# The last expert rows: gated activations as the stationary operand, in two column groups

## The chip, the cores and the metric

The kernel runs on one core of a Trainium2 chip. The metric is the device time of one execution in microseconds. Times inside an execution come from one profiled execution of the kernel before, counted from the start of its span.

## The reference

The reference is one attention block with 16 query heads on one shared key and value head, followed by a block that sends only the 8 best of 2048 rows through a gated expert and adds the result to those rows.

```python
S, D, F, C = 2048, 448, 1792, 8
h = x + softmax(q k^T / sqrt(28)) v @ wo          # on layernorm(x), 16 heads of 28
x2 = layernorm(h)
r = x2 @ w_r
idx = argsort(-r)[:8]
g = silu(x2[idx] @ w_gate)                        # 8 x 1792
u = x2[idx] @ w_up
y = (g * u) @ w_down                              # 8 x 448
out = h + x2
out[idx] += y * sigmoid(r[idx])
```

The change is in the last lines: the product with `w_down`, the sum with the eight residual rows, and the write of the eight sums over their rows of the output.

## The kernel before

The 2048 rows lie as 16 tiles of 128 rows in SBUF. The attention's scores are made in pairs of matmuls into two PSUM banks, and their exponentials are taken by ScalarE (L1012) and in part by VectorE with integer operations (L1024, L1031). The products with the values (`P,Vs` and `Y,Vs` in the trace) go in fours to four column groups of TensorE: each writes 32 partitions of PSUM, beginning at 0, 32, 64 and 96. All TensorE matmuls carry the line of the helper `mm`, L436, so the tiles tell them apart.

The program is written as a graph of operations with durations, priorities, and the keys that they read and write. A planner orders each engine's operations by priority and readiness, and turns the dependences into waits on semaphores. Of an operation's waits, the one that the planner expects last is held by the operation's own first instruction, and the others stand ahead of it as instructions of their own (L289).

The tail begins when the last attention block is done. The last four row tiles are normalised (L964 for the expert's input `xn`, L971 for the output rows `x_sb`). The scores of all rows are compared, and `oh5` holds one-hot columns: for each of the last four tiles, 128 x 8 with a one where a row of the tile is the j-th chosen, and a fifth one for the rows that were gathered from earlier tiles (`extc`, which lies in `xnT`). A product with `oh5` therefore picks the chosen rows. The picked inputs go through `wg_sb` and `wu_sb` in 14 blocks of 128 hidden units; the result, gated and weighted with the sigmoid, is `guT`: 128 hidden units x 8 rows for each of 14 blocks, made in two halves (L1218).

Then the part that is changed. `psy` is a set of four banks, one for each quarter of 112 output columns, and holds the sum transposed: output columns on partitions, the 8 rows as columns. `row_mm` (L1181) makes the chosen residual rows, five matmuls a quarter, with 128 columns of the rows as the stationary operand and 8 one-hot columns moving. The down projection (L1222) adds 56 matmuls, 14 a quarter, with 128 columns of `w_down` stationary and 8 columns of `guT` moving. VectorE copies the quarters in two halves to `yT` (L1230), TensorE transposes them back by matmuls with an identity, and ScalarE (L1236) and VectorE (L1238) copy 224 columns each to `fin`, which lies in the tile `wq_sb`. GpSimd scatters the 8 rows of `fin` to the output with an indirect DMA (L1239).

Of the kernel before, what the change touches and what calls it, by code (L numbers as in the profile page):

```python
# [6 lines left out]
ACT = mybir.ActivationFunctionType  # L7
# [3 lines left out]
BF16 = mybir.dt.bfloat16  # L11
# [6 lines left out]
PE, AC, DV, PO, SP = "pe", "act", "dve", "pool", "sp"  # L18
# [282 lines left out]
def _main(nc, G, sb, ps, psb, flag, scr, xs, ptab, A_x, A_wq, A_wk, A_wv, A_wo, B_w_r, B_w_gate, B_w_up, B_w_down, out,  # L301
          exact=False):
    S, D, H, C = A_x.shape[1], A_x.shape[2], 16, 8
    DH = D // H
    FF = B_w_gate.shape[1]
    NT, NQB, CK, NB = S // 128, S // 512, 112, 16
    NCH, NFC = D // CK, FF // 128
    XW = D + 4
# [13 lines left out]
    ident = sb("ident", [128, 128], BF16)  # L322
    idi = sb("idi", [128, 128], I32)
    x_raw = sb("x_sb", [128, NT * XW + 16], BF16)
    x_sb = x_raw[:, 0:NT * XW].rearrange("p (t d) -> p t d", d=XW)
# [44 lines left out]
    outf = x_sb[:, :, 0:D]  # L370
# [6 lines left out]
    wd_raw = sb("wd_sb", [128, NFC * D + 16], BF16)  # L377
    wd_sb = wd_raw[:, 0:NFC * D].rearrange("p (k n) -> p k n", n=D)
    fin = wq_sb[0:8, 0, :]
# [10 lines left out]
    extc = xnF[:, 3072:3072 + XW + 16]  # L390
# [15 lines left out]
    oh5 = sb("oh5", [128, 5, 8], BF16)  # L406
# [8 lines left out]
    onesh = sb("onesh", [128, 128], F16)  # L415
    pz = sb("pz", [128, 8], F16)
    wlo = sb("wlo", [1, 8], F32)
    yT = sb("yT", [128, NCH, 8], BF16)
    xselT = sb("xselT", [128, NCH, 8], BF16)
    eg = sb("eg", [128, NFC, 8], F32)  # L420
    sg = sb("sg", [128, NFC, 8], F32)
    guT = sb("guT", [128, NFC, 8], BF16)
# [3 lines left out]
    def acc_bank(b):  # L426
        return 6 + b % 2
# [4 lines left out]
    def pk(b):  # L432
        return ("ps", b)

    def mm(o, l, r, start, stop):
        return lambda e: e.matmul(o, lhsT=l, rhs=r, start=start, stop=stop)  # L436
# [25 lines left out]
    for i in range(4, NT, 4):  # L462
        dma(x_sb[:, i:i + 4, 0:D], x_v[:, i:i + 4, :], [("x", t) for t in range(i, i + 4)], lat=3500.0 + 400 * i,
            reads=[("x", 3)])
    G.op(PO, lambda e: e.iota(idi[:, :], [[1, 128]], base=0, channel_multiplier=-1), 250, writes=["idi"])
    G.op(PO, lambda e: e.tensor_single_scalar(ident[:, :], idi[:, :], 0, ALU.is_equal), 560,
         reads=["idi"], writes=["ident"])
    G.op(PO, lambda e: e.memset(nhalf[:, :], -0.5), 100, writes=["nhalf"])
    for _ in range(44):
# [3 lines left out]
         writes=["pid2"])  # L473
    G.op(DV, lambda e: e.tensor_single_scalar(pidx[:, :], pidx[:, :], 31, ALU.bitwise_and), 70, reads=["pidx"],
         writes=["pidx"])
    for p in range(2):
        G.op(DV, lambda e, p=p: e.tensor_scalar(ksc[:, p:p + 1], pid2[:, :], 32, KSCALE,
                                                ALU.is_ge if p else ALU.is_lt, ALU.mult), 70, reads=["pid2"],
             writes=[("ksc", p)])
# [3 lines left out]
         writes=["qone"])  # L483
# [3 lines left out]
    def pad_wq(g, after=()):  # L487
# [5 lines left out]
        else:  # L493
# [4 lines left out]
         reads=["wk_sb", "wk_rep"], writes=["wk_rep"])  # L498
    G.op(PO, lambda e: e.tensor_copy(wv_pad[0:CK, :, 1:1 + DH], wv_sb[0:CK, :, :]), 250,
         reads=["wv_sb", "wv_pad"], writes=["wv_pad"])  # L500
# [7 lines left out]
    def kk(j, p):  # L508
        return ("K0", min(j, 2), p) if j < 4 else ("K", j // 4, p)
# [474 lines left out]
    left = [p for p in first if p not in [q[0:2] for q in EARLY]]  # L984
# [96 lines left out]
    if exact:  # L1081
# [4 lines left out]
        for b in range(NB):  # L1086
            if b >= 2:
                q_project(b, misc_bank(b))
            for i in range(4):
                rows = slice(32 * i, 32 * i + 32)  # L1090
                for k in range(4):
# [4 lines left out]
                         reads=[("Q", b % 4), ("Qh", b % 4)] + [kk(j, i % 2) for j in (0, 2, 4, 8, 12)], writes=[pk(c) for c in range(4)])  # L1096
                    G.op(DV, lambda e, r2=r2: e.tensor_reduce(nmax[:, r2:r2 + 1], ps[:, 0:4, :], AX.XY, ALU.max,
                                                              negate=True), 2200,
                         reads=[pk(c) for c in range(4)], writes=[("nmax", r2)])
                    G.op(DV, lambda e, r2=r2: e.tensor_scalar(nmax[:, r2:r2 + 1], nmax[:, r2:r2 + 1], OCT, None,  # L1100
                                                              ALU.mult), 90,
                         reads=[("nmax", r2)], writes=[("nmax", r2)])
                    G.op(AC, lambda e, r2=r2: e.activation(Pq[:, r2, :], ps[:, 0:4, :].rearrange("p a b -> p (a b)"),
                                                           ACT.Exp, bias=nmax[:, r2:r2 + 1], scale=OCT), 1800,
                         reads=[pk(c) for c in range(4)] + [("nmax", r2)], writes=[("Pq", r2)])
                    for hf in range(2):
# [3 lines left out]
                             reads=[("Pq", r2), "ident"], writes=[pk(bank)])  # L1110
                        G.op(DV, lambda e, bank=bank, hf=hf, r2=r2: e.tensor_copy(
                            PT[:, r2, 8 * hf:8 * hf + 8, :].rearrange("p a b -> p (a b)"), psb[:, bank, :]), 1100,
                            reads=[pk(bank)], writes=[("PT", r2, hf)])
                        G.op(PE, [mm(ps[rows, acc_bank(b), k * 128:(k + 1) * 128], Vs[:, 0, j, :], PT[:, r2, j, :],
                                     j == 0, j == NT - 1) for j in range(8 * hf, 8 * hf + 8)], 600,
                             reads=[("PT", r2, hf)] + [("V", c) for c in range(4)] + ["V1"], writes=[pk(acc_bank(b))])
            post_block(b)
    else:
        events.sort(key=lambda t: t[0])
        for t, fn in events:  # L1120
# [7 lines left out]
         writes=["Ls", "bad1"])  # L1128
    G.op(PE, mm(ps[0:1, 2, 32:33], bad1[:, :], ones128[:, :], True, True), 200, reads=["bad1", "ones128"],
         writes=[pk(2)])  # L1130
    G.op(DV, lambda e: e.tensor_copy(flag[:, :], ps[0:1, 2, 32:33]), 120, reads=[pk(2)], writes=["flag"])
    G.op(DV, lambda e: e.engine_nop() if False else e.tensor_copy(bad1[:, :], bad1[:, :]), 70, reads=["bad1", "flag"],
         writes=["bad1"])
# [4 lines left out]
         writes=[pk(0)])  # L1138
    for k in range(4):
        G.op(PE, mm(ps[0:1, 1, k * 128:(k + 1) * 128], x_sb[:, 12 + k, D + 2:D + 3], ident[:, :], True, True), 100,  # L1140
             reads=[("r", 12 + k), "ident"], writes=[pk(1)])
    G.op(DV, lambda e: e.max(top8[:, 1, :], row), 620, reads=[pk(0), pk(1)], writes=[("top8", 1)])
    G.op(DV, lambda e: e.max_index(idx8[:, 1, :], top8[:, 1, :], row), 700, reads=[pk(0), pk(1), ("top8", 1)],
         writes=[("idx8", 1)])
# [5 lines left out]
        writes=["oh5"])  # L1150
    G.prio = 321
    G.op(AC, lambda e: e.activation(wrow[:, :], top8[:, 1, :], ACT.Exp, scale=-1.0), 200, reads=[("top8", 1)],
         writes=["wrow"])
    G.op(DV, lambda e: e.tensor_scalar(wrow[:, :], wrow[:, :], 1.0, None, ALU.add), 70, reads=["wrow"],
         writes=["wrow"], after=[oh_op])
# [3 lines left out]
         writes=["wlo"])  # L1159
    G.op(DV, lambda e: e.tensor_copy(bz[0:1, 1, :], wlo[:, :]), 90, reads=["wlo", "bz"], writes=["bz3"])  # L1160
    G.op(DV, lambda e: e.tensor_tensor(bz[0:1, 2, :], wlo[:, :], bz[0:1, 1, :], ALU.subtract), 90, reads=["wlo", "bz3"],
         writes=["bz4"])
# [1 line left out]
        last_out(k)  # L1164
    G.prio = 312
    psg = ps[:, 7, 0:NCH * 8].rearrange("p (c j) -> p c j", j=8)
    psy = ps[:, 4:8, 0:8]
    fns = []
    for ch in range(NCH):
        for k in range(4):  # L1170
            o = (12 + k) * D + ch * CK
# [6 lines left out]
         reads=["onesb", "bz", "bz2", "bz3", "bz4"], writes=[pk(7)], prio=321.5)  # L1178
    G.op(DV, lambda e: e.tensor_copy(wbc[:, :], ps[:, 7, 64:72]), 70, reads=[pk(7)], writes=["wbc"], prio=324)

    def row_mm(ch, prio):  # L1181
        fns = []
        for k in range(4):
            o = (12 + k) * XW + ch * CK
            fns.append(mm(psy[:, ch, :], x_raw[:, o:o + 128], oh5[:, k, :], k == 0, False))
        fns.append(mm(psy[:, ch, :], extc[:, ch * CK:ch * CK + 128], oh5[:, 4, :], False, False))
        G.op(PE, fns, 140, reads=["oh5", "extc", "extc2", "x_end"] + [("outf", 12 + k) for k in range(4)] +
             [("r", 12 + k) for k in range(4)], writes=[pk(4 + ch)], prio=prio)

    ps3 = ps[0:8, 2, 480:482]  # L1190
    G.op(PE, [mm(ps3, oh5[:, k, :], x_sb[:, 12 + k, D:D + 2], k == 0, False) for k in range(4)] +
# [1 line left out]
         reads=["oh5", "extc2", ("xi", 0), ("xi", 1)], writes=[pk(2)], prio=313)  # L1193
    G.op(DV, lambda e: e.tensor_copy(sel3[:, :], ps3[:, 1:2]), 70, reads=[pk(2)], writes=["sel3"], prio=318)
    G.op(DV, lambda e: e.tensor_tensor(idxc[:, :], ps3[:, 0:1], sel3[:, :], ALU.add), 70,
         reads=[pk(2), "sel3"], writes=["idxc"], prio=318)
    HF = NFC // 2
    pgu = ps[:, 0:4, 0:HF * 8].rearrange("p b (c j) -> p b c j", j=8)
    for h in range(2):
        fcs = range(HF * h, HF * h + HF)  # L1200
        bg, bu = h, 2 + h
        for w_, nm, bk in ((wg_sb, "wg_sb", bg), (wu_sb, "wu_sb", bu)):
            G.op(PE, [mm(pgu[:, bk, fc - HF * h, :], w_[0:CK, ch, fc * 128:(fc + 1) * 128], xselT[0:CK, ch, :], ch == 0,
                         ch == NCH - 1) for fc in fcs for ch in range(NCH)], 780, reads=[nm, "xselT"],
                 writes=[pk(bk)], prio=320 + bk)
        sl = slice(HF * h, HF * h + HF)
        G.op(DV, lambda e, sl=sl, bg=bg: e.tensor_scalar(eg[:, sl, :], pgu[:, bg, :, :], -43.0, None, ALU.max), 130,
             reads=[pk(bg)], writes=[("eg", h)], prio=320)
        for f, sc, bi in ((ACT.Exp, -1.0, 0.0), (ACT.Ln, 1.0, 1.0), (ACT.Exp, -1.0, 0.0)):
            G.op(AC, lambda e, f=f, sc=sc, bi=bi, sl=sl: e.activation(  # L1210
                eg[:, sl, :], eg[:, sl, :], f, bias=bi, scale=sc), 190,
                reads=[("eg", h)], writes=[("eg", h)], prio=325)
        G.op(DV, lambda e, sl=sl, bg=bg: e.tensor_tensor(sg[:, sl, :], pgu[:, bg, :, :], eg[:, sl, :], ALU.mult), 150,
             reads=[pk(bg), ("eg", h)], writes=[("sg", h)], prio=325)
        G.op(DV, lambda e, sl=sl: e.tensor_tensor(sg[:, sl, :], sg[:, sl, :],
                                                  wbc[:, :].unsqueeze(1).broadcast_to([128, HF, 8]), ALU.mult), 150,
             reads=[("sg", h), "wbc"], writes=[("sg", h)], prio=325)
        G.op(DV, lambda e, sl=sl, bu=bu: e.tensor_tensor(guT[:, sl, :], pgu[:, bu, :, :], sg[:, sl, :], ALU.mult), 150,  # L1218
             reads=[pk(bu), ("sg", h)], writes=[("guT", h)], prio=325)
    for ch in range(NCH):  # L1220
        row_mm(ch, 326 + 0.1 * ch)
    for h in range(2):  # L1222
        for c2 in ((0, 1), (2, 3)):
            G.op(PE, [mm(psy[:, ch, :], wd_raw[:, fc * D + ch * CK:fc * D + ch * CK + 128], guT[:, fc, :], False,
                         fc == NFC - 1) for ch in c2 for fc in range(HF * h, HF * h + HF)], 390,
                 reads=[("guT", h), "wd_sb", "wd_end"], writes=[pk(4 + ch) for ch in c2], prio=327 + h)
    G.prio = 330
    for h in range(2):
        c2 = slice(2 * h, 2 * h + 2)
        G.op(DV, lambda e, c2=c2: e.tensor_copy(yT[0:CK, c2, :], psy[0:CK, c2, :]), 100,  # L1230
             reads=[pk(4 + 2 * h), pk(5 + 2 * h)], writes=[("yT", h)])
    for h in range(2):
        G.op(PE, [mm(ps[0:8, h, ch * CK:(ch + 1) * CK], yT[0:CK, ch, :], ident[0:CK, 0:CK], True, True)
                  for ch in (2 * h, 2 * h + 1)], 200, reads=[("yT", h), "ident"], writes=[pk(h)], prio=329.5 if h == 0 else None)
    hd = D // 2
    G.op(AC, lambda e: e.activation(fin[:, 0:hd], ps[0:8, 0, 0:hd], ACT.Identity), 300, reads=[pk(0)],  # L1236
         writes=["fin0"] + wqs)
    G.op(DV, lambda e: e.tensor_copy(fin[:, hd:D], ps[0:8, 1, hd:D]), 300, reads=[pk(1)], writes=["fin1"])  # L1238
    o = G.op(PO, lambda e: e.indirect_dma_start(out[0], bass.IndirectOffsetOnAxis(ap=idxc[:, 0:1], axis=0),  # L1239
                                                fin[:, :], None), 1000, dma=True,  # L1240
             reads=["fin0", "fin1", "idxc"] + [("out", q, k) for q in range(4) for k in (1, 3)],
             writes=[("out", 4)])
# [4 lines left out]
def bass_sequential_preLN__grouped_kv_mqa__moe_arch_mod__prompt_kernel(  # L1247
# [3 lines left out]
    with es:  # L1251
# [13 lines left out]
        for exact in (False, True):  # L1265
            G = _Graph(sems, dsems, graphs[0] if exact else None)
            with contextlib.ExitStack() as mem:
                def sb(name, shape, dt, mem=mem, pre="x_" if exact else ""):
                    return mem.enter_context(nc.sbuf_tensor(pre + name, shape, dt))
                _main(nc, G, sb, ps, psb, flag, scr, xs, ptab, A_x, A_wq, A_wk, A_wv, A_wo, B_w_r, B_w_gate, B_w_up, B_w_down,  # L1270
                      out, exact)
            graphs.append(G)
# [74 lines left out]
```

## Time and profile before

| | |
|---|---|
| median of 3 runs | 388.9 us (388.54 to 389.18) |
| the profiled execution | 387.67 us |
| its span | 385.9 us |
| mean granted TensorE clock | 0.984 |
| busy: PE, DVE, ACT, POOL | 344.0, 338.2, 374.1, 115.0 us |
| instructions | 8129 |

The span runs from the first to the last instruction; the execution's own time is a little longer. Busy times are sums over the span; `PEld` is TensorE's loading of stationary operands, which goes on beside its matmuls. A shape such as `128*8 128x224` names the rows and columns of the stationary operand and then the moving one. In the order of instructions below, a matmul's row shows the tiles read, moving operand first, and the shape of what it writes.

### The profile page before, as it was taken

What the parts mean: (1) busy time and instruction counts of PE and PEld (TensorE: products, weight loads), DVE (VectorE), ACT (ScalarE), POOL (GpSimd) and SP (SyncE); (2) the same over time, 40 slices, a digit from 0 to 9 for tenths busy, and PEclk for the clock granted to TensorE, in tenths of its full rate; (3) what the DMA queues carried; (4) which work ended last, traced back from release to release, by engine and by line L of the source; (5) the groups of instructions that cost most, each with busy time, mean ns of one, the idle gap of its engine ahead of it and who ended that gap; (6) DMA issues with size and microseconds to landing.
All of it is one profiled execution on the core that took longest, in us unless ns stands there. A gap on an engine that the chain in (4) does not pass through costs nothing.

```text
span 385.9 us, 8129 instructions
## 1 busy us (share of the span) xinstructions
PE 344.0 (89%) x3361; PEld 105.6 (27%) x3361; DVE 338.2 (88%) x613; ACT 374.1 (97%) x433; POOL 115.0 (30%) x149
## 2 busy tenths in 40 slices
PE   7799898989988999899998988999898999888945
PEld 7333222222222222222222222222222222222324
DVE  6985888888998999989999989999999998999382
ACT  6999999999999999999999999999999999999992
POOL 7440002544123112404101244402145454431100
PEclk9999999999999999999999999999999999999985
DMA  8696000100000000201001000011001010100011
GB/s 208 163 235 190 2 2 12 49 2 29 2 27 5 4 29 26 77 1 54 2 14 63 7 27 27 28 50 31 26 30 51 3 53 27 52 26 20 14 51 55
DMA packets 18045, 17.12 MB, mean 44 GB/s; under 512 B 6660, under 2 KB 15124, under 8 KB 18004
## 3 DMA queue, kind: packets, MB, share of 16 engines
q1 hardware_dynamic: 17652, 16.32, 14.7%
q8 instruction: 27, 0.44, 0.5%
q10 hardware_dynamic: 288, 0.23, 0.2%
q14 instruction: 14, 0.11, 0.1%
q0 software_dynamic: 64, 0.02, 0.0%
HBM read 11.70 MB, written 4.86 MB: 43 GB/s over the span
## 4 chain that ended last, share of the span: by engine, by line
ACT 92%; PE 3%; DVE 3%; DMA 1%; issue 0%; SPq 0%; POOL 0%; POOLq 0%
ACT P L1012 90%; PE ps L436 3%; DMA wq_sb<-in_A_wq_dram 1%; ACT xn L964 1%; DVE Y L1024 1%; DVE topb L856 0%; DVE bn L934 0%; SPq L449 0%; ACT x_sb L825 0%; DVE Y L1031 0%; ACT xnT L618 0%; POOL out_dram L1239 0%; ACT Rb L741 0%; ACT Rb L739 0%; ACT wq_pad L491 0%
## 5 line engine op out<-in xcount | busy, mean ns | idle before, releaser
L1012 ACT ACTIVATE P<-ps 128x1024 bf16<-128x1024 f32 x388 | 356.3, 1132 | 1.4 <-PE ps L436 1.3
L436 PE MATMUL ps<-Q,K 64*128 64x512 bf16 x1024 | 179.9, 385 | 29.3 <-ACT P L1012 25.0
L1024 DVE TENSOR_SCALAR Y<-ps 128x1024 int16<-128x1024 f32 x124 | 151.2, 1219 | 19.8 <-PE ps L436 19.5
L1031 DVE TENSOR_SCALAR Y<-Y 128x2048 int16<-128x2048 int16 x153 | 100.4, 685 | 0.5
L436 PEld LDWEIGHTS ps<-Q,K 64*128 64x128 bf16 x1024 | 44.7, 93 | 175.4 <-ACT P L1012 152.7
L1031 POOL TENSOR_SCALAR Y<-Y 128x2048 int16<-128x2048 int16 x33 | 62.6, 1898 | 96.4 <-DVE Y L1031 87.6
L436 PE MATMUL ps<-Y,Vs 128*32 128x512 bf16 x992 | 84.9, 383 | 0.0
L436 PE MATMUL ps<-P,Vs 128*32 128x512 bf16 x776 | 76.3, 388 | 0.1
L767 POOL TENSOR_TENSOR On<-Ot,Rb 128x512 bf16<-128x512 f32 x15 | 19.1, 1273 | 45.5 <-DVE Y L1031 30.6
L436 PEld LDWEIGHTS ps<-Y,Vs 128*32 128x32 bf16 x992 | 23.8, 95 | 27.3 <-issue 17.5
L436 PEld LDWEIGHTS ps<-P,Vs 128*32 128x32 bf16 x776 | 19.6, 93 | 42.5 <-issue 41.7
L763 POOL TENSOR_TENSOR Ls<-Ls,Lc 128x16 f32<-128x16 f32 x15 | 4.2, 280 | 68.2 <-DVE Y L1031 60.9
L436 PE MATMUL ps<-xnT,wq_pad 112*128 112x512 bf16 (+1 forms) x68 | 19.2, 371 | 0.6 <-DVE K L643 0.5
L436 PE MATMUL ps<-wo_pad,On 128*128 128x448 bf16 (+1 forms) x64 | 17.5, 358 | 1.0 <-DVE On L745 1.0
L517 DVE TENSOR_SCALAR Q<-ps,qone 128x512 bf16<-128x512 f32 x15 | 11.0, 734 | 1.7 <-PE ps L436 1.7
L795 POOL TENSOR_TENSOR hbuf<-st,nhalf 128x1 f32<-128x1 f32 x12 | 6.6, 552 | 14.3 <-DVE Y L1031 10.3
L751 DVE COPY Ot<-ps 128x512 f32<-128x512 f32 x15 | 10.3, 684 | 0.7 <-PE ps L436 0.4
L804 DVE SCALAR_TENSOR_TENSOR junk<-hbuf,w_rb 128x448 bf16<-128x448 f32 x12 | 8.1, 677 | 0.0
L789 DVE TENSOR_TENSOR hbuf<-ps,x_sb 128x448 f32<-128x448 f32 x12 | 7.4, 618 | 0.3 <-PE ps L436 0.2
L791 DVE BATCH_NORM_STATS2 bn<-hbuf 128x6 f32<-128x448 f32 x12 | 7.4, 618 | 0.1
L719 DVE TENSOR_SCALAR K<-ps,ksc,kb 128x512 bf16<-128x512 f32 x6 | 4.6, 803 | 3.3 <-PE ps L436 3.3
L1239 POOL DMA_INDIRECT out_dram<-wq_sb,idxc x1 | 0.9, 930 | 20.8 <-DVE wq_sb L1238 20.8
(209 smaller groups left out, 172.1 us busy)
## 6 DMA issues: line engine op xcount, KB each, us to landing
Rb<-h_scr SPq DMA_DIRECT2D x15, 256.0 KB
h_scr<-hbuf SPq DMA_DIRECT2D x12, 225.0 KB, 2.2
out_dram<-x_sb SPq DMA_DIRECT2D x8, 224.0 KB, 2.5
wg_sb<-in_B_w_gate_dram SPq DMA_DIRECT2D x1, 1568.0 KB, 12.2
wu_sb<-in_B_w_up_dram SPq DMA_DIRECT2D x1, 1568.0 KB, 18.7
wd_sb<-in_B_w_down_dram SPq DMA_DIRECT2D x1, 1568.0 KB, 22.1
x_sb<-in_A_x_dram SPq DMA_DIRECT2D x3, 448.0 KB, 5.6
wo_pad<-in_A_wo_dram SPq DMA_DIRECT2D x4, 98.0 KB
```

The lines of the kernel that those rows point to most:

```text
L436: return lambda e: e.matmul(o, lhsT=l, rhs=r, start=start, stop=stop)
L517: G.op(DV, lambda e: e.tensor_scalar(Q[:, b % 4, :], ps[:, bank, :], qone[:, 0:1], None, ALU.add), dvt(512), reads=[pk(bank), "qone"], wri ...
L719: G.op(DV, lambda e, bank=bank, c=c, p=p: e.tensor_scalar(K[:, p, c * 512:(c + 1) * 512], ps[:, bank, :], ksc[:, p:p + 1], kb[:, p:p + 1], ...
L751: G.op(DV, lambda e: e.tensor_copy(Ot[:, rb, :], ps[:, acc_bank(b), :]), dvt(512), reads=[pk(acc_bank(b))], writes=[("Ot", rb)], prio=u - 30)
L767: G.op(PO, lambda e: e.tensor_tensor(On[:, qb % 2, g, :], Ot[:, rb, :], Rb[:, rb, :], ALU.mult), 1270, reads=[("Ot", rb), ("Rb", rb)], wri ...
L789: G.op(DV, lambda e: e.tensor_tensor(h, ps[:, bank, 0:D], x_sb[:, t, 0:D], ALU.add), dvt(D), reads=[pk(bank), ("x", t)], writes=[("h", hr)])
L791: G.op(DV, lambda e: e.bn_stats(bn6[:, t, :], h), dvt(D), reads=[("h", hr)], writes=[("bn6", t)])
L795: G.op(PO, lambda e: e.tensor_tensor(s4, st[:, t, 7:8], nhalf[:, 0:1], ALU.pow), 570, reads=[("st7", t), "nhalf"], writes=[("h4", hr)])
L804: G.op(DV, lambda e: e.scalar_tensor_tensor(junk[:, :], h, s4, w_rb[:, :], ALU.mult, ALU.mult, accum_out=st[:, t, 2:3]), 700, reads=[("h", ...
L1012: marks["exp"] = G.op(AC, lambda e: e.activation(P[:, sl, :, :], ps[:, b0:b0 + 2, :], ACT.Exp, bias=EBIAS, scale=OCT), 905, reads=[pk(b0), ...
L1024: G.op(DV, lambda e: e.tensor_scalar(Y[:, n, 0, p:p + 3:2, :].bitcast(I16), ps[:, 4:6, :], 0.0, 32639.0 - 3 * STEP, ALU.max, ALU.min), 114 ...
L1031: G.op(PO if po else DV, lambda e: e.tensor_scalar(Y[:, n, v, :, :].bitcast(I16), Y[:, n, 0, :, :].bitcast(I16), 1.0, v * STEP, ALU.mult, ...
```

## The change

The sum is no longer made transposed. The one-hot columns and `guT` become the stationary operand, 8 columns wide, and the rows and the weights move, in two halves of 224 output columns. The first half goes to partitions 0 to 7 of bank 4 and the second to partitions 32 to 39 of bank 5, that is to two column groups of TensorE. The sum then has its 8 rows on partitions, so that `yT`, its copies and the transposes go, and ScalarE and VectorE read the two halves directly.

```diff
-    psy = ps[:, 4:8, 0:8]
...
-    def row_mm(ch, prio):
-        fns = []
-        for k in range(4):
-            o = (12 + k) * XW + ch * CK
-            fns.append(mm(psy[:, ch, :], x_raw[:, o:o + 128], oh5[:, k, :], k == 0, False))
-        fns.append(mm(psy[:, ch, :], extc[:, ch * CK:ch * CK + 128], oh5[:, 4, :], False, False))
-        G.op(PE, fns, 140, reads=["oh5", "extc", "extc2", "x_end"] + [("outf", 12 + k) for k in range(4)] +
-             [("r", 12 + k) for k in range(4)], writes=[pk(4 + ch)], prio=prio)
+    HD = D // 2
+    sums = [ps[32 * g:32 * g + 8, 4 + g, 0:HD] for g in range(2)]
+
+    def down(n, left, right):
+        return [mm(sums[g], left, right[:, g * HD:(g + 1) * HD], n == 0, n == 4 + NFC) for g in range(2)]
...
-    for ch in range(NCH):
-        row_mm(ch, 326 + 0.1 * ch)
+    fns = []
+    for k in range(5):
+        fns += down(k, oh5[:, k, :], x_sb[:, 12 + k, 0:D] if k < 4 else extc[:, 0:D])
+    G.op(PE, fns, 470, reads=["oh5", "extc", "extc2"] + [("outf", 12 + k) for k in range(4)] +
+         [("r", 12 + k) for k in range(4)], writes=[pk(4), pk(5)], prio=326)
     for h in range(2):
-        for c2 in ((0, 1), (2, 3)):
-            G.op(PE, [mm(psy[:, ch, :], wd_raw[:, fc * D + ch * CK:fc * D + ch * CK + 128], guT[:, fc, :], False,
-                         fc == NFC - 1) for ch in c2 for fc in range(HF * h, HF * h + HF)], 390,
-                 reads=[("guT", h), "wd_sb", "wd_end"], writes=[pk(4 + ch) for ch in c2], prio=327 + h)
+        fns = []
+        for fc in range(HF * h, HF * h + HF):
+            fns += down(5 + fc, guT[:, fc, :], wd_sb[:, fc, :])
+        G.op(PE, fns, 660, reads=[("guT", h), "wd_sb"], writes=[pk(4), pk(5)], prio=327 + h)
     G.prio = 330
-    for h in range(2):
-        c2 = slice(2 * h, 2 * h + 2)
-        G.op(DV, lambda e, c2=c2: e.tensor_copy(yT[0:CK, c2, :], psy[0:CK, c2, :]), 100,
-             reads=[pk(4 + 2 * h), pk(5 + 2 * h)], writes=[("yT", h)])
-    for h in range(2):
-        G.op(PE, [mm(ps[0:8, h, ch * CK:(ch + 1) * CK], yT[0:CK, ch, :], ident[0:CK, 0:CK], True, True)
-                  for ch in (2 * h, 2 * h + 1)], 200, reads=[("yT", h), "ident"], writes=[pk(h)], prio=329.5 if h == 0 else None)
-    hd = D // 2
-    G.op(AC, lambda e: e.activation(fin[:, 0:hd], ps[0:8, 0, 0:hd], ACT.Identity), 300, reads=[pk(0)],
+    G.op(AC, lambda e: e.activation(fin[:, 0:HD], sums[0], ACT.Identity), 300, reads=[pk(4)],
          writes=["fin0"] + wqs)
-    G.op(DV, lambda e: e.tensor_copy(fin[:, hd:D], ps[0:8, 1, hd:D]), 300, reads=[pk(1)], writes=["fin1"])
+    G.op(DV, lambda e: e.tensor_copy(fin[:, HD:D], sums[1]), 300, reads=[pk(5)], writes=["fin1"])
```

On TensorE the end of the program stands as follows before, from the weighting row's spreading (`bz`) and the up projection (`wu_sb`) to the reading of a flag; `oh` is `oh5`.

```order
L436 MATMUL ps<-bz,onesb 128x8 x3
L436 MATMUL ps<-xselT,wu_sb 128x8 x56
L436 MATMUL ps<-oh,x_sb 128x8 x4
L436 MATMUL ps<-oh,xnT 128x8
...
L436 MATMUL ps<-guT,wd_sb 128x8 x56
L436 MATMUL ps<-ident,yT 8x112 x4
L1284 TENSOR_LOAD flag
```

And in the changed kernel, from the same place on:

```order
L435 MATMUL ps<-bz,onesb 128x8 x3
L435 MATMUL ps<-xselT,wu_sb 128x8 x56
L435 MATMUL ps<-x_sb,oh 8x224 x8
L435 MATMUL ps<-xnT,oh 8x224 x2
L435 MATMUL ps<-wd_sb,guT 8x224 x28
L1274 TENSOR_LOAD flag
```

In place of 20 row matmuls, 56 of the down projection and 4 transposes stand 10 and 28 matmuls of 224 columns. What stands ahead of them is unchanged.

On GpSimd the scatter's waits before are these; `m_act` and `m_dve` are the semaphores of ScalarE and VectorE, `md...` those of DMAs, and the last in the brackets is held by the scatter itself.

```order
L761 TENSOR_TENSOR Lsi<-Lsi,Li 128x16 [waits m_dve]
L767 TENSOR_TENSOR On<-Ot,Rb 128x512 [waits md99,m_dve]
L1284 TENSOR_LOAD flag [waits m_dve]
L1239 DMA out_dram<-wq_sb,idxc 2048x448 [waits md100,md80,md103,md69,md104,md58,md105,md47,m_act,m_dve]
L1295 COMPARE_AND_BRANCH
```

The same place in the changed kernel:

```order
L760 TENSOR_TENSOR Lsi<-Lsi,Li 128x16 [waits m_dve]
L766 TENSOR_TENSOR On<-Ot,Rb 128x512 [waits md99,m_dve]
L1274 TENSOR_LOAD flag [waits m_dve]
L1229 DMA out_dram<-wq_sb,idxc 2048x448 [waits md100,md80,md103,md69,md104,md58,md105,md47,m_dve,m_act]
L1285 COMPARE_AND_BRANCH
```

The two last waits have changed places: VectorE's now stands in an instruction ahead of the scatter, and ScalarE's is held by it.

1 line of the change is left out of this document (removed).

## The prediction

> **What bounds the kernel now.** I read the page first, for the span, the clock and the chain that ended last.
>
> ```profile
> span 385.9 us, 8129 instructions
> ...
> PEclk9999999999999999999999999999999999999985
> ...
> ACT 92%; PE 3%; DVE 3%; DMA 1%; issue 0%; SPq 0%; POOL 0%; POOLq 0%
> ```
>
> ScalarE's exponentials carry 92% of the chain, but the change lies behind them, so only the end of the chain matters. The granted clock falls in the last two of 40 slices, where the change lies. The chain in order of time shows which engine holds that end.
>
> ```profile
> 349.28 16.61 ACT P L1012 x18
> ...
> 375.61 5.53 PE ps L436 x193
> 381.14 0.02 issue
> 381.16 0.35 ACT wq_sb L1236
> ```
>
> From 375.61 to 381.14 the end hangs on TensorE alone. ScalarE's first half of the result closes there by the profile, but it is VectorE's second half that ends last, as the timeline of that stretch shows. Its columns are start, duration, engine, line, operation and tiles; a row with a count merges instructions, and its duration runs from the first start to the last end.
>
> ```profile
> 378.66 0.18 PEld L436 LDWEIGHTS ps<-oh,x_sb 128*128 128x128 bf16 x4
> 378.68 0.22 DVE L1215 TENSOR_TENSOR sg<-sg,wbc 128x56 f32<-128x56 f32 x1
> 378.68 0.25 PE L436 MATMUL ps<-oh,x_sb 128*128 128x8 bf16 x4
> ...
> 378.93 0.22 DVE L1218 TENSOR_TENSOR guT<-ps,sg 128x56 bf16<-128x56 f32 x1
> ...
> 379.21 1.64 PE L436 MATMUL ps<-guT,wd_sb 128*128 128x8 bf16 x56
> 380.51 0.17 DVE L1230 CAST yT<-ps 112x16 bf16<-112x16 f32 x1 [1.37 <-PE ps L436]
> 380.78 0.69 PE L436 MATMUL ps<-ident,yT 112*8 112x112 bf16 x4
> 380.89 0.17 DVE L1230 CAST yT<-ps 112x16 bf16<-112x16 f32 x1 [0.20 <-PE ps L436]
> 381.11 0.09 PEld L436 LDWEIGHTS ps<-ident,yT 112*8 112x8 bf16 x2 [0.25 <-DVE yT L1230]
> 381.16 0.35 ACT L1236 ACTIVATE wq_sb<-ps 8x224 bf16<-8x224 f32 x1 [2.77 <-PE ps L436]
> 381.50 0.38 DVE L1238 CAST wq_sb<-ps 8x224 bf16<-8x224 f32 x1 [0.44 <-PE ps L436]
> 382.45 0.93 POOL L1239 DMA_INDIRECT out_dram<-wq_sb,idxc  x1 [20.80 <-DVE wq_sb L1238]
> ```
>
> The residual rows start at 378.68 and the down projection at 379.21. Its inputs guT are complete at 378.93 + 0.22 = 379.15, so TensorE does not wait for them: this stretch is as long as TensorE's own stream. Behind it come a copy, two transposes and the result's second half, which ends at 381.88; the scatter follows. The windows give the clock that was granted meanwhile (after the dots: engine busy times, then PEclk).
>
> ```profile
> 374.60:378.66 4.06, 3.94 (x140) 3.85 (x141) 2.52 (x16) 3.67 (x10) 0.00 (x0) 0.50 0.34 113
> 378.66:380.85 2.19, 2.19 (x85) 2.17 (x81) 0.61 (x3) 0.00 (x0) 0.00 (x0) 0.50 0.07 19
> 380.85:381.88 1.03, 0.61 (x4) 0.11 (x4) 0.55 (x2) 0.35 (x1) 0.00 (x0) 0.50 0.00 0
> ```
>
> The whole end runs at a granted clock of 0.50, and 4 us of back-to-back 8-column matmuls did not bring it back.
>
> **What is removed.** Of the rows and the down projection 20 + 56 = 76 matmuls go, each with 8 moving columns behind a 128-column load. The 56 take 1.64 us with the last one's own 0.168 (the mean of its group, below), so they are (1.64 - 0.168) / 55 = 26.8 ns apart, even at half clock; 20 rows in 379.21 - 378.68 = 0.53 us give 26.5 ns. Then go the two yT copies and the four transposes. From the first row at 378.68 to the start of the last copy at 381.50 all this is 2.82 us.
>
> ```profile
> L436 PE MATMUL ps<-guT,wd_sb 128*128 128x8 bf16 x56 | 1.6, 168 | 0.0
> ```
>
> **What is added.** Now 5 + 14 = 19 pairs of matmuls, each with 224 moving columns behind an 8-column load; a pair's two matmuls go to two column groups of the array. Three things set the price: the rate per column at this clock, whether the two overlap, and the way into the column groups. For the rate I take the start of the kernel, where matmuls of 128 columns run back to back.
>
> ```profile
> 1.88 2.95 PE L436 MATMUL ps<-ident 128*128 128x128 bf16 x26 [1.88 <-POOL ident L466]
> ...
> 4.63 1.25 PE L436 MATMUL ps<-ident 128*128 128x128 bf16 x18
> ...
> L436 PE MATMUL ps<-ident 128*128 128x128 bf16 x26 | 3.0, 313 | 1.9 <-POOL ident L466 1.9
> ```
>
> The first 26 are (2.95 - 0.313) / 25 = 0.1055 us apart, the later ones about (1.25 - 0.22) / 17 = 0.061: the slow rate is 0.824 ns a column. The transposes at the end confirm which rate holds there: the last two, of 112 columns each, run from 381.11 to 380.78 + 0.69 = 381.47, 0.36 us; less the 0.168 that a short matmul takes to pass, this leaves 0.19, or 0.86 ns a column. VectorE starts 0.03 behind them. So 224 columns cost 0.185 us at a clock of 0.50. For the overlap I take the attention's products, which use four column groups.
>
> ```profile
> 360.98 0.60 PE L436 MATMUL ps<-Y,Vs 128*32 128x512 bf16 x8
> ...
> 375.14 0.17 PE L436 MATMUL ps<-oh,xnT 128*128 128x8 bf16 x1
> ...
> 375.24 0.14 PEld L436 LDWEIGHTS ps<-x_sb,oh 128*8 128x8 bf16 x4
> 375.24 0.24 PE L436 MATMUL ps<-x_sb,oh 128*8 128x2 bf16 x4
> ...
> L436 PE MATMUL ps<-Y,Vs 128*32 128x512 bf16 x992 | 84.9, 383 | 0.0
> ```
>
> Eight of them take 0.60 us, and one alone 0.383: the second four come 0.217 us after the first four. So four of 512 columns pass in the time of one, at 0.424 ns a column and full clock, and their loads cost nothing. I take a pair as one matmul of 224 columns. The way into column groups costs 375.24 - 375.14 = 0.10 us instead of 0.027, where 8-column loads follow 128-column ones; I add 0.07.
>
> Sum: the first pair starts at 378.75, the last 18 x 0.185 = 3.33 us later at 382.08; it ends 0.185 + 0.168 later at 382.43, and with the 0.03 of signal both halves of the result start at 382.46. VectorE's takes 0.38 as before and ends at 382.84, against 381.88: **0.96 us later**. ScalarE's half, earlier hidden by 0.37, now runs beside it, 0.35 against 0.38.
>
> **The scatter's wait.** Before, GpSimd's queue waits for ScalarE in an instruction of its own and then for VectorE in the scatter itself; now the scatter itself waits for ScalarE, and the instruction ahead of it for VectorE. The earlier gather and the scatter itself price the passage; the first in the timeline.
>
> ```profile
> 352.62 0.08 DVE L874 TENSOR_SCALAR idc<-posc 8x1 uint32<-8x1 f32 x1
> ...
> 353.06 1.27 POOL L882 DMA_INDIRECT xnT<-h_scr,idc  x1 [1.29 <-DVE idc L874]
> ```
>
> The chain in order of time has the queue's part before the scatter.
>
> ```profile
> 381.52 0.03 POOLq L289
> 381.55 0.64 issue
> ```
>
> The gather starts 353.06 - 352.70 = 0.36 us behind VectorE when its queue had long been through its other waits. The scatter starts 0.57 behind VectorE (382.45 - 381.88) and 0.90 behind its wait for ScalarE at 381.55. If the 0.57 is VectorE's, nothing changes; if the 0.90 is the time from the instruction ahead, VectorE now pays it with 0.03 more, and the end moves 0.36. A gain is excluded, since no wait is taken away. Neither row decides; I take the middle, 0.18.
>
> All else is covered: the yT copies' absence frees VectorE, which waits anyway; TensorE's reading of the flag behind its last matmul moves by 1 us under a scatter that lasts until 383.38 and lands later. The order ahead of 378.66 is the same but for a branch hint's place. So the end moves by 0.96 + 0.18 = 1.14 us. The profiled execution took 387.67 us against a span of 385.9 and should become 388.8; the median of the three runs is 388.9, 1.2 above it, and becomes 390.0 to 390.1; I say 390.1.
>
> **The rivals.**
>
> First, the clock comes back while the pairs stream. At the start dense matmuls from 1.88 brought the fast rate near 4.8, 2.9 us later; here dense work from 378.75 would bring it at 381.65, with 382.27 - 381.65 = 0.62 us still to stream, which halves: 0.3 us less, 389.8. Against a much earlier return stand the windows at 0.50 above; for it, that 224 columns fill the array and 8 did not. I give it 0.22, its returns spread over the stretch, so that two thirds of it end within 0.78 us of before. The Trainium skill's page "TensorE: Matmul & The Clock Gate", Part 1, tells of a gate that halves the clock and lifts it after one busy window of about 3.4 us, on a grid that runs free of the kernel; the trace agrees with the halving (0.1055 against 0.061 us), and by that rule, as an estimate from the page, a return anywhere in the stretch is as likely as another.
>
> Second, and on the other side: the clock is full early. It has its place at 378.75, where the first pair starts. With all 19 pairs at 224 x 0.424 = 0.095 us, the last starts at 378.75 + 1.71 = 380.46, and the result ends at 380.46 + 0.095 + 0.168 + 0.03 + 0.38 = 381.13, 0.75 us early; less 0.18 for the scatter this is 0.57 faster, 388.3. It decides from a return at T where (382.27 - T) / 2 = 1.14, so T = 379.99: back by then, the kernel is not slower. For it speaks that dense matmuls did lift it once; against it, that this took 2.9 us and not 1.2, and that the clock stood at 0.50 through the 4 us ahead. 0.12.
>
> Third, the two groups take turns: 19 x 0.185 = 3.5 us more, 393.6. Against it stands the row of eight products. 0.05.
>
> Fourth, the 8-column loads are not hidden. Four took 0.14 us, at most 0.035 each; 38 are 1.3 us more, 391.4. Against it: the loads of 32 columns cost nothing above, under longer matmuls though. 0.07. The Trainium skill's page "TensorEngine Tiling (Array Packing)", Restrictions and Gotchas, says that column tiling excludes the fast weight load; no run here shows what that costs at 8 columns.
>
> **How the numbers follow.** The forecast has 0.54. About 0.2%, 0.78 us, is what a measurement of this kernel can tell from no change. Slower by more: of the forecast, which ends 0.96 to 1.32 later by the scatter's two prices, 0.49 (0.05 are for its other sizes), the third and fourth rivals, 0.12, and the late third of the first, 0.07: 0.68. Within 0.78: the other 0.15 of the first, 0.05 of the second and 0.05 of the forecast, 0.25. Faster by more: a full clock with nothing paid at the scatter and a little more, 0.07. The range runs from a return of the clock just after 380, at 389.0, to exposed loads at 391.4; it leaves out the second rival and the third, 0.17.
>
> **What would show it.** In the timeline of the changed kernel: 10 and 28 matmuls of 224 columns from 378.7 to about 382.4 in pairs that start together, pairs 0.185 apart, with a granted clock of 0.50; VectorE's half starting near 382.46, the scatter 0.57 to 0.94 behind its end. Pairs 0.095 apart, a clock of 1.00 there, or the scatter starting before 382.45 would make the forecast wrong; matmuls 0.185 apart one by one would be the third rival.

## The result, and the profile after

In 22 runs each, taken in turn on the same chip, the changed kernel took a median of 389.27 us and the kernel before 388.51. The ratio is 1.0019, with a 95% interval of 1.0011 to 1.0028: the change costs about 0.75 us (0.4 to 1.1). The time lies in the range forecast, near its lower end. But the move is two thirds of the 1.14 us in the sum, and the kernel before also came out 0.39 us lower in 22 runs than in the three that the forecast started from.

The profiled execution of the changed kernel took 389.13 us with a span of 387.2. Its stage, in the timeline (start, duration, engine, line, operation, tiles):

```profile
379.25 0.91 PE L435 MATMUL ps<-x_sb,oh 128*8 128x224 bf16 x8
379.43 0.22 DVE L1213 TENSOR_TENSOR guT<-ps,sg 128x56 bf16<-128x56 f32 x1
379.76 0.13 PEld L435 LDWEIGHTS ps<-xnT,oh 128*8 128x8 bf16 x2
379.95 0.40 PE L435 MATMUL ps<-xnT,oh 128*8 128x224 bf16 x2
...
380.14 2.82 PE L435 MATMUL ps<-wd_sb,guT 128*8 128x224 bf16 x28
383.00 0.35 ACT L1226 ACTIVATE wq_sb<-ps 8x224 bf16<-8x224 f32 x1 [4.16 <-PE ps L435]
383.00 0.38 DVE L1228 CAST wq_sb<-ps 8x224 bf16<-8x224 f32 x1 [3.36 <-PE ps L435]
384.33 0.93 POOL L1229 DMA_INDIRECT out_dram<-wq_sb,idxc  x1 [22.61 <-DVE wq_sb L1228]
```

The 28 matmuls stand in 14 pairs: (2.82 - 0.392) / 13 = 0.187 us apart, with 0.392 the mean of one from the groups by shape. Both halves of the result start together at 383.00, 3.75 us behind the first row; before it was 381.50 - 378.68 = 2.82. The windows give the clock in that stretch:

```profile
379.25:383.00 3.75, 3.71 (x41) 2.35 (x38) 0.31 (x2) 0.00 (x0) 0.00 (x0) 0.50 0.02 7
```

It was 0.50, as forecast. The chain's last pieces (start, duration, what) show the scatter's wait:

```profile
383.00 0.39 DVE wq_sb L1228
383.40 0.03 POOLq L289
383.43 0.64 issue
384.07 0.08 POOLq L1285
384.15 0.19 issue
384.33 0.93 POOL out_dram L1229
```

The scatter starts 0.95 us behind VectorE's end at 383.38, not 0.58. From its wait ahead, over at 383.43, it is 0.90 us, as it was from ScalarE's wait before (381.55 to 382.45).

So far the changed kernel loses 5.08 - 3.77 = 1.31 us from the first row to the scatter's start. Part of it comes back behind it. The DMA view over the 2 us from the scatter's start, first of the kernel before and then of the changed one, lists the packets of each queue, and the issue with its median time to landing:

```profile
q14 instruction: 2, 0.02, 3.1%
q8 instruction: 1, 0.02, 2.8%
q0 software_dynamic: 32, 0.01, 1.7%
issues: line engine op xcount, KB each, median us to landing
out_dram<-wq_sb,idxc POOLq DMA_INDIRECT x1, 2.9
```

```profile
q0 software_dynamic: 32, 0.01, 1.6%
q14 instruction: 1, 0.01, 1.5%
...
out_dram<-wq_sb,idxc POOLq DMA_INDIRECT x1, 2.4
```

Before, a fetch of 16 KB of code on queue 8 starts in these 2 us, 0.68 us behind the scatter's start, and the scatter lands 2.90 us behind its start. After the change the fetch starts 0.65 us ahead of the scatter, and the scatter lands at 2.37. The fetch is put down to TensorE, because it starts 0.59 to 0.66 us behind the first instruction after TensorE's jump to the end in 13 of the 14 traces below (0.94 in this one of the kernel before). The sum from the first row to the landing is 3.77 + 2.90 = 6.67 us before and 5.08 + 2.37 = 7.45 after. The difference is 0.78. Ahead of the first row 0.07 more go to the way into the column groups: 0.097 us pass there from the last matmul of the up projection, and 0.027 before. Together this is 0.85, inside the 0.4 to 1.1 that the runs measured.

### The profile page after: what moved, and what is told of

Same layout as the page of the kernel before. It is cut to its first block, busy times and chain, and to the rows that moved or that the text cites. A ratio compares the mean times of both kernels' runs of the same rounds, so it can differ in the third digit from the quotient of the medians.

```text
span 387.2 us, 8043 instructions
## 1 busy us (share of the span) xinstructions
PE 345.7 (89%) x3319; PEld 106.5 (27%) x3319; DVE 337.8 (87%) x611; ACT 374.3 (97%) x433; POOL 115.5 (30%) x149
## 4 chain that ended last, share of the span: by engine, by line
ACT 90%; PE 5%; DVE 3%; POOL 0%; issue 0%; POOLq 0%
ACT P L1011 90%; PE ps L435 5%; DVE Y L1023 1%; DVE topb L855 0%; DVE bn L933 0%; ACT x_sb L824 0%; DVE Y L1030 0%; POOL out_dram L1229 0%; PE ps L438 0%; ACT Rb L740 0%; DVE idx L1142 0%; DVE top L1141 0%; ACT Rb L738 0%; POOL ident L465 0%; DVE On L744 0%
```

## The experiments

Each ratio is against the kernel before, run in turn on the same chip. The theory after the result: the pairs at half clock cost 1.0 us and the scatter's wait 0.37, and 0.55 come back because TensorE's last code fetch no longer delays the scatter's landing. Rivals: the clock has no part in it; the wait is VectorE's; the landing is chance.

**Four column groups.**

```diff
-    HD = D // 2
-    sums = [ps[32 * g:32 * g + 8, 4 + g, 0:HD] for g in range(2)]
+    HD = D // 4
+    sums = [ps[32 * g:32 * g + 8, 4 + g, 0:HD] for g in range(4)]
```

> The changed kernel with four column groups of 112 columns in place of two of 224 (banks 4 to 7), and two copies each on ScalarE and VectorE. If the clock of 0.50 and the columns per group set the price: four matmuls start together, the fours stand 0.093 us apart in place of 0.187, the last four begins 1.68 us behind the first in place of 3.36, the copies cost 0.25 more, and the time falls by about 1.4 us below the changed kernel, to 0.7 below before. If the groups take turns beyond two, or the loads of 8 columns (now 76) set the pace, the fours stand 0.19 or more apart and nothing is gained.

Measured: 388.59 us, ratio 0.9999 (0.9986 to 1.0011). The timeline of this kernel:

```profile
379.87 1.52 PE L435 MATMUL ps<-wd_sb,guT 128*8 128x112 bf16 x56
381.45 0.52 ACT L1230 ACTIVATE wq_sb<-ps 8x112 bf16<-8x112 f32 x2 [2.40 <-PE ps L435]
381.45 0.56 DVE L1233 CAST wq_sb<-ps 8x112 bf16<-8x112 f32 x2 [1.60 <-PE ps L435]
382.95 0.93 POOL L1234 DMA_INDIRECT out_dram<-wq_sb,idxc  x1 [20.77 <-DVE wq_sb L1233]
```

The fours are (1.52 - 0.299) / 13 = 0.094 us apart (0.299 is the mean of one), half of the pairs' 0.187, and the scatter starts 3.50 us behind the first row at 379.45, 0.27 sooner than before and 1.58 sooner than in the changed kernel. The columns per group at this clock set the price, and neither turns nor loads. But only about 0.8 of the expected 1.4 us below the changed kernel is seen, and the time is level with before. In this trace the scatter lands 3.5 us behind its start, with the code fetch in between; the view covers 2 us from that start:

```profile
q8 instruction: 1, 0.02, 3.5%
q14 instruction: 1, 0.01, 1.6%
q0 software_dynamic: 30, 0.01, 1.5%
...
out_dram<-wq_sb,idxc POOLq DMA_INDIRECT x1, 3.5
```

Only 30 of the scatter's 32 packets are in these 2 us. The same view from 2.20 to 2.40 us behind the start has the other two:

```profile
q0 software_dynamic: 2, 0.00, 1.4%
```

They start at 2.27 and 2.28 us, where the fetch ends (2.28). In the traces without a late fetch all 32 have started by 1.72.

**TensorE kept busy in its idle time**, in the changed kernel and in the one before:

```diff
+    def busy(n, prio, after):
+        if not exact:
+            G.op(PE, [mm(ps[:, 7, 128:256], ident[:, :], ident[:, :], True, True) for _ in range(n)], 56 * n,
+                 reads=["ident"], writes=[pk(7)], prio=prio, after=after)
...
+            busy(30, 301, [lp])
...
+    busy(22, 310.5, [sc_op, bad_op])
...
+    busy(4, 311, [pz_op])
```

> The changed kernel with 56 matmuls of 128 columns on the identity added, whose result nobody reads, in TensorE's idle time between the last projection and the expert (30, 22 and 4 of them). If the clock is what costs: it stays at 1.00 up to the down projection, the pairs stand 0.095 us apart in place of 0.187, the last pair begins 1.70 behind the first, and the time is 1.7 us below the changed kernel, 0.9 below before. If the clock is not kept by them, or falls again under the 8-column matmuls, the pairs stay 0.187 apart. If the price lies in something else than the clock, the clock is 1.00 and the time stays at 0.7 above before.

> The kernel before with the same 56 added matmuls, as the counterpart: what the full clock alone is worth there. Its 76 matmuls of 8 columns are 26.8 ns apart at half clock, and loads of 128 columns set that pace; at full clock 25 ns at best, so 0.1 us less, with the passage of matmuls and transposes perhaps 0.3 less in all. If the clock helped it as much as the changed kernel (1.7 us), the clock would not be what tells the two apart.

Measured: 388.57 us, ratio 0.9989 (0.9974 to 1.0003), for the changed kernel, and 388.47, ratio 0.9990 (0.9980 to 1.0001), for the one before. The windows of the changed kernel, ahead of the pairs and in them:

```profile
376.00:379.70 3.70, 3.61 (x140) 3.49 (x136) 2.17 (x15) 3.49 (x10) 0.00 (x0) 1.00 0.33 113
379.90:383.10 3.20, 3.20 (x38) 2.29 (x34) 0.43 (x2) 0.00 (x0) 0.00 (x0) 0.50 0.04 10
```

The clock stays up through the gate and up projections and falls just as the pairs begin, although TensorE was recorded busy for 3.61 of the 3.70 us ahead. So this did not try what it was meant to. But the trace has the price of 8-column matmuls at a full clock, in the up projection:

```profile
378.26 1.54 PE L435 MATMUL ps<-xselT,wu_sb 112*128 112x8 bf16 x56
```

With 0.166 for the last one they are (1.54 - 0.166) / 55 = 25.0 ns apart at 1.00, against 26.7 at 0.50 in the kernel before: their distance hardly depends on the clock. The pairs were still at 0.50; the clock came back at 383.21, 0.17 us ahead of the last one's end. The two kernels came out level here, 388.57 and 388.47. Their traces are 0.52 us apart from the first row to the landing (7.10 and 6.58), which the width of the two intervals does not exclude.

**The scatter's waits in the order of before, in the changed kernel.**

```diff
-    G.op(AC, lambda e: e.activation(fin[:, 0:HD], sums[0], ACT.Identity), 300, reads=[pk(4)],
+    G.op(AC, lambda e: e.activation(fin[:, 0:HD], sums[0], ACT.Identity), 200, reads=[pk(4)],
```

> The changed kernel with the planner's duration of ScalarE's last copy at 200 in place of 300, which gives the scatter its waits in the order of before: ScalarE's in the instruction ahead, VectorE's held by the scatter. If it is the place of VectorE's wait that costs: the scatter starts 0.58 us behind VectorE's end in place of 0.95, and the time falls by 0.37. If 0.9 us pass from the end of the wait ahead, whoever is waited for there: ScalarE ends only 0.04 earlier than VectorE, the scatter starts 0.91 behind VectorE, and nothing is gained.

Measured: 389.22 us, ratio 1.0014 (1.0002 to 1.0025). The chain:

```profile
383.42 0.35 ACT wq_sb L1226
383.77 0.03 POOLq L289
...
384.71 0.93 POOL out_dram L1229
```

VectorE's copy ends at 383.80, and the scatter starts 0.91 behind it, again 0.91 behind the wait ahead at 383.80. The place of VectorE's wait is not what costs. The scatter's start follows the end of the last wait ahead, whoever is waited for, and in the changed kernel both halves end together, so that nobody is early.

**The code of four groups shifted.**

```diff
+    busy(18, 310.5, [sc_op, bad_op])
```

> The kernel with four groups and 18 unread matmuls of 128 columns more in an idle time of TensorE some 5 us earlier, which move its code so that its jump to the end comes as early as in the kernels that jump at once. If TensorE's last code fetch, 0.60 us behind its jump, is what made the scatter of four groups land late (3.46 us behind its start, one of 16 completions late): the fetch is over before the scatter's packets (1.5 us behind its start), it lands 2.1 to 2.4 behind, and the time falls by about 1.1 us below four groups, to 0.9 to 1.2 below before. If the late landing is chance or the scatter's own: still near 3.4 or scattered, and the time stays level with before.

Measured: 388.36 us, ratio 0.9995 (0.9980 to 1.0010). In the trace the fetch comes 0.40 us behind the scatter's start in place of 1.18, and the scatter lands at 2.45 in place of 3.46, as the theory has it:

```profile
q8 instruction: 1, 0.02, 2.7%
...
q0 software_dynamic: 32, 0.01, 1.6%
...
out_dram<-wq_sb,idxc POOLq DMA_INDIRECT x1, 2.5
```

The median is 0.2 us below before, where 0.9 to 1.2 was expected; the interval ends at 0.8. So one trace has the gain, and the times don't show it.

**The waits swapped in the kernel before.**

```diff
-    G.op(AC, lambda e: e.activation(fin[:, 0:hd], ps[0:8, 0, 0:hd], ACT.Identity), 300, reads=[pk(0)],
+    G.op(AC, lambda e: e.activation(fin[:, 0:hd], ps[0:8, 0, 0:hd], ACT.Identity), 700, reads=[pk(0)],
```

> The kernel before with the planner's duration of ScalarE's last copy at 700 in place of 300, which alone swaps the scatter's two waits: VectorE's in the instruction ahead, as in the changed kernel. If 0.91 us pass from the end of the wait ahead: the scatter starts 0.95 behind VectorE in place of 0.58, 0.37 later. If TensorE's code fetch delays two of its completions before: it is now over when the packets go, the scatter lands 2.1 to 2.4 behind its start in place of 2.9, and in sum the kernel is 0.1 to 0.4 us faster or level, though its scatter starts later. If the landing has nothing to do with the fetch: 2.9 again, and 0.37 us slower.

Measured: 388.63 us, ratio 0.9999 (0.9982 to 1.0015): level, though the interval also holds 0.37 us. The trace tells the two apart:

```profile
382.75 0.38 DVE L1238 CAST wq_sb<-ps 8x224 bf16<-8x224 f32 x1 [0.44 <-PE ps L436]
384.07 0.93 POOL L1239 DMA_INDIRECT out_dram<-wq_sb,idxc  x1 [21.33 <-DVE wq_sb L1238]
...
out_dram<-wq_sb,idxc POOLq DMA_INDIRECT x1, 2.5
```

The scatter starts 0.95 us behind VectorE's end, 0.37 later than in the unchanged kernel, and lands 2.45 behind its start in place of 2.90: the later start costs nothing.

**Dense work inside the gate and up projections**, with the added matmuls above, in both kernels:

```diff
+                if (fc - HF * h) % 2 and not exact:
+                    fns.append(mm(ps[:, bk, 256:512], ident[:, :], wd_sb[:, 0, 0:256], True, True))
```

> The changed kernel with the 56 unread matmuls and 12 more of 256 columns inside the gate and up projections, so that the array stays busy there too; they cost about 1.3 us ahead of the change. If the clock stays at 1.00: pairs 0.095 us apart, the last pair 1.70 behind the first in place of 3.36. If the clock is not what sets the pairs' distance: 0.187 at a clock of 1.00.

> The kernel before with the same added matmuls, as the counterpart. At a clock of 1.00 its 76 matmuls stand 25 to 26 ns apart in place of 26.8. From the first row to the end of VectorE's last copy it then takes about 2.9 us in place of 3.2, and the changed kernel 2.4 in place of 4.1: with 0.37 lost at the scatter the changed kernel would be level with it or up to 0.6 us faster, where it is 0.7 slower at a clock of 0.50.

Measured: 390.70 us, ratio 1.0050 (1.0032 to 1.0068), changed, and 389.69, ratio 1.0029 (1.0013 to 1.0045), before. The clock fell again, at 376.7 in the changed kernel's trace, so that the times don't compare the two at full clock. But it came back inside the pairs, and this trace has both rates in one stretch:

```profile
382.16 0.77 PE L435 MATMUL ps<-wd_sb,guT 128*8 128x224 bf16 x6
...
383.28 1.05 PE L435 MATMUL ps<-wd_sb,guT 128*8 128x224 bf16 x16
...
381.25:382.70 1.45, 1.45 (x21) 1.03 (x19) 0.21 (x1) 0.00 (x0) 0.00 (x0) 0.50 0.00 0
...
383.60:384.30 0.70, 0.70 (x16) 0.43 (x10) 0.00 (x0) 0.00 (x0) 0.00 (x0) 1.00 0.00 0
```

The first three pairs take 0.77 us, 0.187 apart at a clock of 0.50. The clock rose at 383.51. The step between pairs in which it rose is 0.119, and the last five are 0.096 at 1.00. The clock does set the pairs' distance: at full clock it is half, where 8-column matmuls gain 1.7 ns of 26.7. The other kernel's profiled execution took 394.71 us, 5 above its median. Its chain was held up in the loads at the start, and its rows and down projection ran at 0.50 as well, so the trace has nothing at 1.00 to compare.

**The flag read early, before the change.**

```diff
-                place = G.flag_place(eng)
+                place = G.early.idx if eng == PE else G.flag_place(eng)
```

> The kernel before with TensorE's reading of the flag (0.48 us, behind its last matmul) moved into a wait of TensorE some 7 us earlier, so that its jump to the end comes about 0.5 us sooner. If its last code fetch, 0.60 us behind the jump, delays completions of the scatter: the fetch now starts about 0.2 us behind the scatter's start in place of 0.7 and is over before the packets at 1.5; the scatter lands 2.1 to 2.4 behind its start in place of 2.9, and the time falls by 0.4 to 0.8 us. If the late landing is not the fetch's: 2.9 and no change.

Measured: 388.54 us, ratio 1.0006 (0.9993 to 1.0018). A miss, in that the edit did not move what it was to move: TensorE's branch behind it took longer. Its duration before, and here:

```profile
L1295 PEldq COMPARE_BRANCH  x1: 473/473/473, 381.7 to 381.7; - x1
```

```profile
L1295 PEldq COMPARE_BRANCH  x1: 1237/1237/1237, 381.8 to 381.8; - x1
```

The fetch came 0.56 us behind the scatter's start in place of 0.68, and the landing stayed at 2.78. What that branch waits for, the profile doesn't name.

**Three copies on ScalarE, one on VectorE, with four groups.**

```diff
-        if g < 2:
+        if g < 3:
             G.op(AC, lambda e, f=f, g=g: e.activation(f, sums[g], ACT.Identity), 220, reads=[pk(4 + g)],
```

> Four groups with three copies on ScalarE and one on VectorE, for whom the instruction ahead of the scatter waits, and the flag read early as well. If 0.91 us pass from the end of the wait ahead: the scatter starts about 0.95 behind VectorE's single copy, 3.2 us behind the first row in place of 3.50 with two and two and 3.77 before. With the fetch over before the packets it lands at 2.1 to 2.4, and the kernel is 0.7 to 1.1 us faster than before. If the fetch meets the packets again, it lands at 2.7 to 3.5 and is level with before.

Measured: 388.77 us, ratio 1.0005 (0.9992 to 1.0018). The timeline:

```profile
381.57 0.79 ACT L1230 ACTIVATE wq_sb<-ps 8x112 bf16<-8x112 f32 x3 [2.33 <-PE ps L435]
381.57 0.28 DVE L1233 CAST wq_sb<-ps 8x112 bf16<-8x112 f32 x1 [1.58 <-PE ps L435]
382.79 0.93 POOL L1234 DMA_INDIRECT out_dram<-wq_sb,idxc  x1 [20.92 <-ACT wq_sb L1230]
```

The scatter starts 0.95 behind VectorE's single copy and 0.43 behind ScalarE's last, 3.22 us behind the first row. From the end of the wait ahead it is 0.91 us here too. But the fetch began 1.14 behind the scatter's start, it landed at 3.19, and the gain was gone, as the expectation's last sentence has it.

**Both kernels once more**, unchanged.

> The kernel before, unchanged, for a second trace. If the parts found in its first trace are its own and not one execution's: 3.77 us from the first row to the scatter's start, 0.58 from VectorE's last copy to it, and a landing 2.8 to 2.9 behind it with TensorE's last fetch 0.3 to 0.9 behind it. If the landing is chance: anything from 2.0 to 3.5.

> The changed kernel, unchanged, for a second trace and more times. If its parts are its own: 5.05 to 5.09 us from the first row to the scatter's start, 0.95 from VectorE's copy to it, a landing 2.0 to 2.4 behind it, in sum 7.4 to 7.5 from the first row to the landing against 6.6 to 6.7 before, and a time 0.6 to 0.9 us above before. If the landing is chance and the sum is 1.3 longer, the time is 1.3 above.

Measured: one run of the kernel before, 389.07 us; the changed kernel 388.97, ratio 1.0015 (1.0006 to 1.0024). Before: 3.78 us from the first row to the scatter, and 2.91 to the landing. Changed: 5.09 and 2.32. In sum 6.69 and 7.41, 0.72 apart; the first traces gave 0.78. The parts are each kernel's own.

The landings of all 14 traces, beside the end of the 16 KB fetch, in us from the scatter's start and in order of the fetch (below 0 it ended ahead of that start):

```text
kernel                      fetch   landing
changed, busy               -1.03    2.08
changed, dense              -0.30    2.10
changed again               -0.03    2.32
changed                      0.43    2.37
changed, waits               0.58    2.37
four groups, shifted         1.27    2.45
before, waits swapped        1.33    2.45
before again                 1.46    2.91
before                       1.58    2.90
before, flag early           1.59    2.78
before, busy                 1.68    2.80
four, three and one          2.07    3.19
four groups                  2.28    3.46
before, dense                2.67    3.76
```

The scatter's packets go from 1.5 us behind its start. A fetch that is over by 1.33 leaves the landing at 2.1 to 2.45. One that ends at 1.46 or later moves it with it, to 1.1 to 1.5 us behind the fetch. The two need not meet, though: in "before again" the fetch was over 0.03 us ahead of the first packet, and the landing was late all the same, so what exactly holds up the completions stays open there. In two kernels the order of the two was moved by an edit (the shifted code and the swapped waits), and the landing followed both times; in "four groups" and "four, three and one" two packets start only when the fetch ends (2.28 and 2.07). The 8 KB fetches on queue 14 are not the cause, since they are over by 1.45 in every trace, with late landings and without.

The times agree without proving it: in all eight comparisons but the busy and dense ones, the change in the sum from first row to landing, with the 0.07 where operands are turned, lies inside the interval that was measured, but these intervals are 0.7 to 1.3 us wide. In the late landings one to three of the 16 completions are late and the others in time. The Trainium skill's page "DMA: Bandwidth & Descriptors", section "Why a DMA increments its semaphore by 16 and not by 1", says that each of the 16 engines posts a completion of its own for such a DMA; the trace agrees, with 13 to 16 of them within 2.3 us in every run. The trace does not name a packet's engine, so that the late ones are of the engine that carries the fetch is not shown, though the two late packets of "four groups" point to it.

## Why the prediction was right and wrong

The way it would go was right, and so was what it rests on: 0.50 as the clock, pairs that start together 0.187 us apart (0.185 forecast), loads of 8 columns that cost nothing, and 4.13 us from the first row to the end of VectorE's copy, where the steps gave 382.84 - 378.75 = 4.09. Against 3.20 before, and with 0.07 for the way in, that term is 1.00; the sum had 0.96.

The scatter's wait was mis-sized by the choice of the middle, 0.18. It is 0.37, the upper end: the row that carried it was the 0.90 us behind the wait ahead, and not the 0.57 behind VectorE. All 14 traces have 0.91 behind that wait, while the time behind the engine for which the scatter itself waits runs from 0.43 to 1.3.

The step that failed is the sentence "All else is covered", where "TensorE's reading of the flag behind its last matmul moves by 1 us under a scatter that lasts until 383.38 and lands later". It put the landing at the same time behind the scatter before and after, without a row for it. The reading itself moved the other way. Its row before, and after:

```profile
L1284 PEldq TENSOR_LOAD <-flag x1: 488/488/488, 381.1 to 381.1; - x1
```

```profile
L1274 PEldq TENSOR_LOAD <-flag x1: 490/490/490, 380.7 to 380.7; - x1
```

This is 2.43 us behind the first row before and 1.47 after, well ahead of the last pair, which starts 3.32 behind it. The branch that follows takes 1.75 us in place of 0.47, and the code fetch comes at nearly the same time behind the first row: 4.45 and 4.25 us in the two traces before, 4.44 and 4.09 in the two after. But the scatter starts 1.31 later, and so the fetch that, by the runs above, held up its landing before is over in time. The landing is 2.90 and 2.91 behind the scatter's start before, 2.37 and 2.32 after: about 0.55 come back, which the sum had at nothing. 1.00 + 0.37 - 0.55 = 0.82 is left of the 1.37 that its own terms would have made, close to the 0.75 measured.

That the forecast's 1.14 is no further off is in part luck: the 0.19 that it had too little for the wait took off part of the 0.55 that it had too much for the landing. Of the 0.8 us between the 390.1 forecast and the 389.27 measured, 0.39 lie in the median of three runs from which it started.

The first rival, a clock that comes back in the stretch, was not seen in the changed kernel's two traces. In the one with dense work it came back 2.24 us behind the first row, which shows its price, and in the one kept busy 3.48 behind it, when nearly all had passed. The second did not occur, and what a full clock from the first pair is worth stays an estimate, since no run kept it: 18 steps of 0.187 - 0.096 us are 1.6 us less for the pairs, against 0.1 for the 76 matmuls before. The third and fourth are refuted by the pairs' and the fours' distances.

## What to carry to other kernels

Ask which clock is granted in a short tail, and which of the matmuls there depend on it: 76 matmuls of 8 moving columns passed at 27 ns each at half clock, and those of the up projection at 25 at full clock, while the same sums with 224 columns moving cost 187 ns a pair at half clock and 96 at full clock. At half clock turning the operands brought the scatter's start forward only with fewer columns per group (four groups halved the price, and the time was then level with before). Count the end of a kernel to the last landing, with the code fetches in it, and not to the last engine's work: a gain of 0.3 us at the scatter's start was lost again in a trace where a fetch ended behind its packets. And let the result that an indirect DMA waits for last be held by the DMA itself, with the waits ahead of it over early.

## What was not expected of the hardware

TensorE recorded as busy doesn't mean that its clock is kept: with 3.61 us of 3.70 busy, most of it in 8-column matmuls, the clock fell right after. With 256-column matmuls mixed in it fell 0.9 us into the gate projection and stayed at 0.50 through the rest of both projections. It came back twice, both times while pairs of 224 columns streamed. The scatter of GpSimd starts 0.91 us behind the end of the wait ahead of it in all 14 traces; its packets go from 1.5 us behind its start in every trace, and its completions come from 1.8 us on. A 16 KB code fetch that ends 1.46 us behind its start or later goes with a landing at 2.8 to 3.8, and one that is over by 1.33 with 2.1 to 2.45.
